# Retention products on the full 128x128 array, with one mask operation per head pair

## The chip, the cores and the metric

One core of a Trainium2 chip runs the whole program as one launch. The metric is device time in microseconds, the median of several runs. TensorE multiplies, VectorE (DVE), ScalarE (ACT) and GpSimd (POOL) do the elementwise work, and SyncE (SP) issues nearly all DMAs. TensorE's results land in PSUM, in banks of 512 fp32 columns.

## The reference, cut to what matters

A retention layer (a linear recurrence with one decay per head) feeds two FFNs in a row.

```python
batch, n_heads, seq, head_dim = (4, 8, 768, 64)
gamma = 1.0 - 2.0 ** (-5.0 - np.arange(H, dtype=np.float32))
for t in range(S):
    state = gamma[None, :, None, None] * state + np.einsum('bhd,bhe->bhde', k[:, :, t], v[:, :, t])
    y[:, :, t] = scale * np.einsum('bhd,bhde->bhe', q[:, :, t], state)
...
x = attn_out.transpose(0, 2, 1, 3).reshape(B * S, H * D)      # 3072 tokens of 512
h = x @ w_in;  g = where(h > 0, h, exp(min(h, 0)) - 1);  x = g @ w_out          # first FFN, 512 -> 2048 -> 512
h = x @ w_in2; g = P(h) / (Q(h) + 1e-6);                 out = g @ w_out2       # second FFN
```

The weights arrive as float64 words, which the kernel turns to fp32 itself.

## The kernel before, in words

**Retention in chunks.** Each sequence of 768 steps is cut into 6 chunks of C = 128, so there are 24 chunks. A chunk has 4 *items*, one for each pair of heads; item i is chunk i // 4, pair i % 4, 96 items in all. With two heads of 64 features, a pair fills the 128 partitions. For an item TensorE makes, all in fp32:

- the *kv sum* (L189): decayed keys times values of the pair, 128x128, of which the two diagonal 64x64 blocks are used; left out in the last chunk of a sequence;
- the *scores* (L196): for each head, keys times queries of its 64 partitions, so with half of the array's rows. The two heads write to two PSUM banks, `pa` and `pb`;
- the *state product* (L223): the state `St` of both heads (block diagonal) times the queries, into the output tile `so`; left out in the first chunk of a sequence;
- the *output products* (L225): for each head its values times its masked scores, into its 64 partitions of `so`, so with half of the array's columns.

Between scores and output VectorE masks the scores of each head (L209: times a decay per row, times the triangle). `at_state` updates `St` from the kv sum, and `at_x` splits `so` into a high and a low part, `xh` and `xl`, which are the FFN's input.

**Order.** It is written out by hand; each engine takes its instructions as they were emitted. First come 16 items alone (the *opening*, chunks 0 to 3), while the first weights are converted. Then the first FFN runs over NB = 6 token blocks j and KF = 16 slices f: twelve matmuls of 512 columns make `h` (`g1`), and twelve more accumulate into `acc` (`g2`, for the slice before). One item is woven into each of the first 80 of these steps: its state and output products stand behind `g1`, and the kv sum and scores of the next item behind `g2`. Block 0 converts the first FFN's weights on the way (L106 to L110 on VectorE, L120 on GpSimd); blocks 1 to 4 convert the second FFN's. Block 5 and the second FFN have no retention.

**Loads.** After the last item of a chunk has its scores, `load_k` issues keys, keys for the kv sum and values of the next chunk on SP (L152 to L154). From chunk 4 on, `kT` and `kn` have one buffer each and the values have two. GpSimd multiplies `kn` by its decay (`scale_k`, L163) before the next kv sum.

Of the kernel before, what the change touches and what calls it, by code (L numbers as in the profile page):

```python
# [17 lines left out]
H = 8  # L18
S = 768
D = 64  # L20
# [27 lines left out]
def retention_ffn_kernel(ctx: ExitStack, tc: tile.TileContext, qkT, kv, w1i, w1o, w2i, w2o, a_, b_, tab, out):  # L48
# [26 lines left out]

# [1 line left out]
    W = {}  # L77
# [36 lines left out]
    def split_w(ph, f, e):  # L114
        c = W.pop((ph, f, e, "c"))
        nm = "io"[e]
        hi = wp.tile([128, 512], F32R, tag=f"{nm}h{f}", name=f"{nm}h{f}")
        lo = wp.tile([128, 512], F32R, tag=f"{nm}l{f}", name=f"{nm}l{f}")
# [5 lines left out]
    tab_t = acon.tile([128, tab.shape[1]], F32, name="tab_t")  # L124
# [4 lines left out]
    tri_t = tab_t[:, 532:532 + C]  # L129
    St = acon.tile([128, NP, 128], F32, name="St")  # L130

    def chunk_bufs(alloc):
        kT, kn = alloc("kT"), alloc("kn")
        return kT.rearrange("p (a t) -> p a t", a=NP), kn.rearrange("p (h d) -> p h d", h=H)

    chk = {}

    def load_q(c):
        if c in (2, 3):
            qT, vn, kT, kn = (wp.tile([128, 512], F32, tag=next(late), name=nm) for nm in ("qT", "vn", "kT", "kn"))  # L140
            qT, kT = (t.rearrange("p (a t) -> p a t", a=NP) for t in (qT, kT))
            vn, kn = (t.rearrange("p (h d) -> p h d", h=H) for t in (vn, kn))
        else:
            qT = atw.tile([128, NP, C], F32, tag="qT", name="qT")
            vn = atw.tile([128, H, D], F32, tag="vn", name="vn")
            kT, kn = cb[1 if c == 1 else 0]
        nc.sync.dma_start(out=qT, in_=qkT[c, :, 0])
        chk[c] = (qT, vn, kT, kn)

    def load_k(c):  # L150
        qT, vn, kT, kn = chk[c]
        nc.sync.dma_start(out=kT, in_=qkT[c, :, 1])  # L152
        nc.sync.dma_start(out=kn, in_=kv[c, :, 0])
        nc.sync.dma_start(out=vn, in_=kv[c, :, 1])  # L154

    def scale_q(c, eng):
        qT, vn, kT, kn = chk[c]
        eng.tensor_tensor(out=qT, in0=qT, in1=gq_t, op=ALU.mult)

    def scale_k(c):  # L160
        qT, vn, kT, kn = chk[c]
        if c % CB != CB - 1:
# [12 lines left out]
    def at_in(i, early=False):  # L175
        c, p = divmod(i, NP)
        qT, vn, kT, kn = chk[c]
        if early:
            pa, pb = (psh.tile([128, 512], F32, tag="h", name="sc") if i % 3 == 2 else
                      psa.tile([128, 512], F32, tag=f"acc{2 * (i % 3) + e}", name="sc") for e in range(2))  # L180
        else:
            pa = pst.tile([128, 256], F32, tag="sc", name="sc")
            if p % 2 == 0:
                so_t[0] = pst.tile([128, 3, C], F32, tag="so", name="so")
            pb = so_t[0][:, 2, :]
        ps_t[i] = (pa, pb)
# [12 lines left out]

    def at_mask(i, early=False):  # L200
        p = i % NP
        if early and i % 2:
            A = wp.tile([128, 2, C], F32, tag="ih14", name="A1")
        else:
            A = atw.tile([128, 2, C], F32, tag="A", name="A", bufs=1)
        A_t[i] = A

        def part(e):
            nc.vector.scalar_tensor_tensor(out=A[:, e, :], in0=ps_t[i][e][:, 0:C], scalar=gi_t[:, 2 * p + e:2 * p + e + 1],  # L209
                                           in1=tri_t, op0=ALU.mult, op1=ALU.mult)  # L210

        return [lambda: part(0), lambda: part(1)]

    def at_out(i, early=False):
        c, p = divmod(i, NP)
        qT, vn, kT, kn = chk[c]
        A = A_t.pop(i)
        if early and p % 2 == 0:
            so_t[1] = (pst.tile([128, 3, C], F32, tag="so", name="so") if i % 4 else
                       pst.tile([128, 2, C], F32, tag="sc", name="so"))  # L220
        o = so_t[1 if early else 0]
        if c % CB:
            nc.tensor.matmul(out=o[:, p % 2, :], lhsT=St[:, p, :], rhs=qT[:, p, :], start=True, stop=False)  # L223
        for e in range(2):
            nc.tensor.matmul(out=o[64 * e:64 * e + 64, p % 2, :], lhsT=vn[:, 2 * p + e, :], rhs=A[:, e, :],  # L225
                             start=(c % CB == 0), stop=True)

    def at_state(i):
        c, p = divmod(i, NP)
        kv_ps = ps_t.pop(i)[0]  # L230

        def part(e):
            r = slice(64 * e, 64 * e + 64)
            src = kv_ps[r, C + 64 * e:C + 64 + 64 * e]
            dst = St[r, p, 64 * e:64 * e + 64]
# [9 lines left out]

    def at_x(i, early=False):
        c, p = divmod(i, NP)
        if p % 2:
            o = so_t[1 if early else 0]
            xh, xl = x_tile(c // 4)  # L250
# [35 lines left out]

# [1 line left out]
    def gemm3(ps, pairs, first, last):  # L288
# [66 lines left out]

# [1 line left out]
    ctx.enter_context(tc.manual_schedule())  # L357

    nc.scalar.preload_act_table_set("natural_log_exp_and_others")
    cb = [chunk_bufs(lambda nm: acon.tile([128, 512], F32, name=nm))]  # L360
    late = iter(("ih15", "il15", "ih13", "il13", "ih12", "il12", "ih11", "il11", "oh15", "ol15"))
    cb.append(chunk_bufs(lambda nm: wp.tile([128, 512], F32, tag=next(late), name=nm + "1")))
    nc.gpsimd.memset(St, 0.0)
# [17 lines left out]
    lnb = const.tile([128, 2], F32, name="lnb")  # L381
    warm = gp.tile([128, 512], F32R, tag="gl", name="warm")
    nc.vector.memset(warm.bitcast(F32), 0.0)
    wps = psa.tile([128, 512], F32, tag="acc0", name="wps")
    for _ in range(NW):
        nc.tensor.matmul(out=wps, lhsT=warm[:, 0:128], rhs=warm, start=True, stop=True)
    nc.vector.memset(lnb[:, 0:1], QC * TINY)
    nc.vector.memset(lnb[:, 1:2], -LN2_63)
    scale_q(0, nc.vector)
    scale_k(0)  # L390
    scale_q(1, nc.gpsimd)
    conv_ops = []
    for i in range(4 * NP):
        c, p = divmod(i, NP)
        at_in(i, True)
        a = at_mask(i, True)
        a[0]()
        if conv_ops:
            conv_ops.pop(0)()
        a[1]()  # L400
        if i:
            at_out(i - 1, True)
            run(at_state(i - 1))
            at_x(i - 1, True)
        if p == 0 and c:
# [14 lines left out]
    run(at_state(4 * NP - 1))  # L420
    at_x(4 * NP - 1, True)
    narrow_a(0, 1, 1)
# [18 lines left out]
    for j in range(NB):  # L441
        last = j == NB - 1
        for f in range(KF):
# [6 lines left out]
            x1 = narrow_b(0, f + 1, 1) if conv1 else [lambda: None] * 4  # L450
            a = at_mask(nx[0]) if not last else [lambda: None] * 2
            st = [lambda: None] * 2
# [6 lines left out]
            else:  # L459
                x2 = [lambda: None] * 4  # L460
            x1[0](), a[0](), x1[1](), a[1]()
            if not last:
# [47 lines left out]

# [1 line left out]
    at.close()  # L512
# [103 lines left out]
```

## Time and profile before

| | |
|---|---|
| median of 3 runs | 1241.63 us (1241.39 to 1242.66) |
| profiled execution: its span, first to last instruction | 1243.3 us |
| TensorE matmul busy | 1220.0 us, 98% of the span |
| VectorE busy | 800.3 us, 64% |
| ScalarE busy | 648.1 us, 52% |
| GpSimd busy | 420.0 us, 34% |
| mean granted TensorE clock | 0.991 |

Busy shares are means over stages with different limits. Matmul records overlap one another, so a full TensorE row says that it did not wait, not that the array streamed all the time. The profile gives no time outside the span for the profiled execution, which lies 1.7 us above the median of the runs.

### The profile page before, as it was taken

To read this page: it belongs to the slowest core of one execution; us is meant where nothing else is said; L and a number is where in the kernel's file an instruction comes from. 1 tells how busy PE (TensorE), PEld (TensorE's weight loads), DVE (VectorE), ACT (ScalarE), POOL (GpSimd) and SP (SyncE) were. 2 spreads that over 40 slices of the span, in tenths; PEclk is the share of its full clock that TensorE was granted. 3 is DMA by queue.
4 is the path that set the end of the run, shared out by engine and by line. 5 is a ranking of instruction groups with operands and counts; after the bars stand their busy time and mean duration, and the time that the engine had idled before them with its cause. 6 is when DMAs were issued, how large, how long until landed. Compare 5 with 4: busy or idle time off the path is not lost.

```text
span 1243.3 us, 15558 instructions
## 1 busy us (share of the span) xinstructions
PE 1220.0 (98%) x5708; PEld 969.9 (78%) x5708; DVE 800.3 (64%) x1348; ACT 648.1 (52%) x1098; POOL 420.0 (34%) x328
## 2 busy tenths in 40 slices
PE   9888899999999999999999999999999999999998
PEld 6666677777777777777788888888888888888887
DVE  6899964444444544445311188788888888888775
ACT  2444443333333333333345587776776776777665
POOL 3455542322222222232247743223233232233222
PEclk9899899999999999999999999999999999999999
DMA  6354422223332332322224320020020100100000
GB/s 238 120 170 153 153 98 99 85 89 125 110 110 86 126 103 85 119 85 85 102 94 119 106 73 1 1 69 1 1 69 1 54 15 1 60 9 1 34 1 35
DMA packets 41389, 95.73 MB, mean 77 GB/s; under 512 B 4704, under 2 KB 4832, under 8 KB 41312
## 3 DMA queue, kind: packets, MB, share of 16 engines
q1 hardware_dynamic: 41024, 94.39, 23.4%
q8 instruction: 45, 0.74, 0.2%
q10 hardware_dynamic: 288, 0.34, 0.1%
q14 instruction: 32, 0.26, 0.1%
HBM read 73.74 MB, written 20.97 MB: 76 GB/s over the span
## 4 chain that ended last, share of the span: by engine, by line
PE 91%; DVE 6%; issue 1%; DMA 0%; ACT 0%; SPq 0%
PE h L290 42%; PE acc L290 41%; PE sc L196 3%; PE so L225 3%; DVE wc L108 2%; PE sc L189 2%; DVE wc L110 1%; PE so L223 1%; DVE wc L106 1%; DVE wc L107 1%; DVE A L209 0%; DMA vn<-in_kv_dram 0%; DVE St L241 0%; DVE t L479 0%; PE so L196 0%
## 5 line engine op out<-in xcount | busy, mean ns | idle before, releaser
L290 PE MATMUL h<-xh,ih 128*128 128x512 f32 x768 | 310.8, 405 | 0.0
L290 PE MATMUL h<-xh,il 128*128 128x512 f32 x768 | 302.6, 394 | 0.0
L290 PE MATMUL h<-xl,ih 128*128 128x512 f32 x768 | 302.5, 394 | 0.0
L545 POOL TENSOR_TENSOR gl<-e,gh 128x512 fp32r<-128x512 f32 x96 | 124.9, 1301 | 350.0 <-ACT gh L544 212.0
L483 POOL TENSOR_TENSOR gl<-t,gh 128x512 fp32r<-128x512 f32 x96 | 123.5, 1286 | 348.7 <-ACT gh L482 295.8
L466 ACT ACTIVATE t<-h 128x512 f32<-128x512 f32 x96 | 57.4, 598 | 287.5 <-PE h L290 284.7
L290 PEld LDWEIGHTS h<-xh,ih 128*128 128x128 f32 x768 | 145.8, 190 | 38.1 <-ACT gh L482 0.2
L290 PEld LDWEIGHTS h<-xh,il 128*128 128x128 f32 x768 | 145.8, 190 | 31.2
L290 PEld LDWEIGHTS h<-xl,ih 128*128 128x128 f32 x768 | 146.1, 190 | 28.3
L290 PE MATMUL acc<-gh,oh 128*128 128x512 f32 x384 | 158.9, 414 | 0.0
L290 PE MATMUL acc<-gh,ol 128*128 128x512 f32 x384 | 150.5, 392 | 0.0
L290 PE MATMUL acc<-oh,gh 128*128 128x512 f32 x384 | 149.4, 389 | 0.0
L290 PE MATMUL acc<-ol,gh 128*128 128x512 f32 x384 | 149.4, 389 | 0.0
L519 ACT ACTIVATE s<-h 128x512 f32<-128x512 f32 x96 | 57.4, 598 | 136.9 <-PE h L290 136.9
L479 DVE SCALAR_TENSOR_TENSOR t<-t,h 128x512 f32<-128x512 f32 x96 | 65.5, 682 | 85.7 <-ACT t L467 84.9
L482 ACT CAST gh<-t 128x512 fp32r<-128x512 f32 x96 | 59.6, 621 | 103.9 <-DVE t L479 103.9
L209 DVE SCALAR_TENSOR_TENSOR A<-sc,tab_t 128x128 f32<-128x128 f32 x112 | 38.6, 348 | 111.2 <-PE so L196 106.6
L525 DVE SCALAR_TENSOR_TENSOR u<-s,b,u 128x512 f32<-128x512 f32 x96 | 72.0, 750 | 56.0 <-ACT u L520 55.4
L290 PE MATMUL acc<-gl,oh 128*128 128x512 f32 x384 | 103.4, 391 | 0.0
L290 PE MATMUL acc<-oh,gl 128*128 128x512 f32 x384 | 103.1, 389 | 0.0
L535 DVE SCALAR_TENSOR_TENSOR e<-e,ab,r 128x512 f32<-128x512 f32 x96 | 72.1, 751 | 32.0 <-ACT r L529 32.0
L290 PEld LDWEIGHTS acc<-gh,oh 128*128 128x128 f32 x384 | 72.0, 187 | 26.2 <-issue 13.5
(61 smaller groups left out, 2003.6 us busy)
## 6 DMA issues: line engine op xcount, KB each, us to landing
st<-in_w1i_dram SPq DMA_DIRECT2D x16, 512.0 KB, 3.5
st<-in_w1o_dram SPq DMA_DIRECT2D x16, 512.0 KB, 3.5
st<-in_w2i_dram SPq DMA_DIRECT2D x16, 512.0 KB, 5.4
w2s<-wc SPq DMA_DIRECT2D x32, 256.0 KB, 2.0
st<-in_w2o_dram SPq DMA_DIRECT2D x16, 512.0 KB, 3.6
wc<-w2s SPq DMA_DIRECT2D x32, 256.0 KB, 2.7
qT<-in_qkT_dram SPq DMA_DIRECT2D x24, 256.0 KB, 4.4
kT<-in_qkT_dram SPq DMA_DIRECT2D x24, 256.0 KB, 2.7
```

The costliest lines, as they stand in the source:

```text
L196: nc.tensor.matmul(out=ps[:, 0:C], lhsT=kT[r, p, :], rhs=qT[r, p, :], start=True, stop=True)
L209: nc.vector.scalar_tensor_tensor(out=A[:, e, :], in0=ps_t[i][e][:, 0:C], scalar=gi_t[:, 2 * p + e:2 * p + e + 1], in1=tri_t, op0=ALU.mult, ...
L225: nc.tensor.matmul(out=o[64 * e:64 * e + 64, p % 2, :], lhsT=vn[:, 2 * p + e, :], rhs=A[:, e, :], start=(c % CB == 0), stop=True)
L290: nc.tensor.matmul(out=ps, lhsT=lh, rhs=rh, start=first and idx == 0, stop=last and idx == len(pairs) - 1)
L466: nc.scalar.activation(out=t, in_=h, func=ACTF.Relu, scale=-1.0)
L479: nc.vector.scalar_tensor_tensor(out=t, in0=t, scalar=-1.0, in1=h, op0=ALU.add, op1=ALU.max)
L482: nc.scalar.copy(gh, t)
L483: nc.gpsimd.tensor_tensor(out=gl, in0=t, in1=gh.bitcast(F32), op=ALU.subtract)
L519: nc.scalar.activation(out=s, in_=ps, func=ACTF.Square)
L525: nc.vector.scalar_tensor_tensor(out=u, in0=s, scalar=b1, in1=u, op0=ALU.mult, op1=ALU.add)
L535: nc.vector.scalar_tensor_tensor(out=e, in0=e, scalar=ab[:, 0:1], in1=r, op0=ALU.add, op1=ALU.mult)
L545: nc.gpsimd.tensor_tensor(out=gl, in0=e, in1=gh.bitcast(F32), op=ALU.subtract)
```

## The change

Keys and values of a pair are kept in tiles twice as wide, in which each head has its own 128 columns (keys) or 128 rows' worth of columns (values), and the other head's half is zero. The zeros are written once, at the start (`wide_k` on GpSimd, `wide_v` on VectorE); the loads fill only the other parts, in two DMAs for the keys and two for the values, in place of one each. With them every product takes all 128 rows and columns: scores contract over 128 partitions, of which 64 are zero for the other head, and the two output products of a pair accumulate into the same 128 partitions. Both heads' scores stand side by side in one PSUM bank together with the kv sum, so that the mask of a pair is one operation of 128 x 256, by a table `mask` of 8 x 128 columns that is built once. The kv sum reads the values' two used parts out of the wide tile.

Also changed: the output tile is taken by `at_out` and not by `at_in`; the opening uses five PSUM banks for scores in turn, where it used three pairs; a weight's high and low part share one tile; ten more warm-up matmuls; a smaller scratch for dynamic DMA.

```diff
+    mask = acon.tile([128, H, C], F32, name="mask")
+
+    def wide_k(t):
+        t = t.rearrange("p (a e t) -> p a e t", a=NP, e=2)
+        for e in range(2):
+            r = slice(64 - 64 * e, 128 - 64 * e)
+            nc.gpsimd.memset(t[r, :, e, :], 0.0)
+        return t
+
+    def wide_v(t):
+        t = t.rearrange("p (a e d) -> p a e d", a=NP, e=2)
+        for e in range(2):
+            nc.vector.memset(t[:, :, e, 64 - 64 * e:128 - 64 * e], 0.0)
+        return t
...
     def load_k(c):
-        qT, vn, kT, kn = chk[c]
-        nc.sync.dma_start(out=kT, in_=qkT[c, :, 1])
+        qT, vw, kw, kn = chk[c]
+        for e in range(2):
+            r = slice(64 * e, 64 * e + 64)
+            nc.sync.dma_start(out=kw[r, :, e, :], in_=qkT[c, r, 1])
         nc.sync.dma_start(out=kn, in_=kv[c, :, 0])
-        nc.sync.dma_start(out=vn, in_=kv[c, :, 1])
+        for e in range(2):
+            nc.sync.dma_start(out=vw[:, :, e, 64 * e:64 * e + 64],
+                              in_=kv[c, :, 1].rearrange("p (a e) d -> p a e d", e=2)[:, :, e, :])
...
-                nc.tensor.matmul(out=pa[:, C:2 * C], lhsT=kn[:, 2 * p:2 * p + 2, :], rhs=vn[:, 2 * p:2 * p + 2, :],
+                v2 = vw[:, p].rearrange("p e d -> p (e d)").rearrange("p (f d) -> p f d", d=64)[:, 0:4:3, :]
+                nc.tensor.matmul(out=ps[:, 2 * C:3 * C], lhsT=kn[:, 2 * p:2 * p + 2, :], rhs=v2,
                                  start=True, stop=True)
...
-        for e, ps in enumerate((pa, pb)):
-            r = slice(64 * e, 64 * e + 64)
-            nc.tensor.matmul(out=ps[:, 0:C], lhsT=kT[r, p, :], rhs=qT[r, p, :], start=True, stop=True)
+        for e in range(2):
+            nc.tensor.matmul(out=ps[:, e * C:e * C + C], lhsT=kw[:, p, e, :], rhs=qT[:, p, :], start=True, stop=True)
...
-        def part(e):
-            nc.vector.scalar_tensor_tensor(out=A[:, e, :], in0=ps_t[i][e][:, 0:C], scalar=gi_t[:, 2 * p + e:2 * p + e + 1],
-                                           in1=tri_t, op0=ALU.mult, op1=ALU.mult)
-
-        return [lambda: part(0), lambda: part(1)]
+        nc.vector.tensor_tensor(out=A, in0=ps_t[i][:, 0:2 * C].rearrange("p (e t) -> p e t", e=2),
+                                in1=mask[:, 2 * p:2 * p + 2, :], op=ALU.mult)
...
         for e in range(2):
-            nc.tensor.matmul(out=o[64 * e:64 * e + 64, p % 2, :], lhsT=vn[:, 2 * p + e, :], rhs=A[:, e, :],
-                             start=(c % CB == 0), stop=True)
+            nc.tensor.matmul(out=o[:, p % 2, :], lhsT=vw[:, p, e, :], rhs=A[:, e, :],
+                             start=(c % CB == 0 and e == 0), stop=(e == 1))
...
+    for n in (256, 384):
+        for _ in range(5):
+            nc.tensor.matmul(out=wps[:, 0:n], lhsT=warm[:, 0:128], rhs=warm[:, 0:n], start=True, stop=True)
...
+    for h in range(H):
+        nc.vector.tensor_scalar_mul(mask[:, h, :], tri_t, gi_t[:, h:h + 1])
```

On TensorE, in one step of block 0 (each step of blocks 1 to 4 reads alike), an item stands so before; one row of the two FFN products is shown at each border.

```order
L290 MATMUL acc_606<-gl,oh_387 128x512
L189 MATMUL sc<-vn,kn 128x128
L196 MATMUL sc<-qT,kT 128x128
L196 MATMUL so<-qT,kT 128x128
L290 MATMUL h<-xh,ih_538 128x512
...
L223 MATMUL so<-qT,St 128x128
L225 MATMUL so<-A,vn 64x128 x2
L290 MATMUL acc_603<-gh,oh_521 128x512
```

And so after the change, where k_136, v_137 and n_139 are the wide keys, the wide values and the keys of the kv sum:

```order
L298 MATMUL acc_598<-gl,wo_397 128x512
L201 MATMUL sc<-v_137,n_139 128x128
L207 MATMUL sc<-qT,k_136 128x128 x2
L298 MATMUL h<-xh,wi_534 128x512
...
L231 MATMUL so<-qT,St 128x128
L233 MATMUL so<-A,v_137 128x128 x2
L298 MATMUL acc_595<-gh,wo_518 128x512 x2
```

The number of calls and their places are the same; the output products have 128 rows where they had 64, and both scores go to `sc`.

On SP, the first chunk's loads and the start of the next chunk's before:

```order
L147 DMA qT<-in_qkT_dram 128x512
L152 DMA kT<-in_qkT_dram 128x512
L153 DMA kn<-in_kv_dram 128x512
L154 DMA vn<-in_kv_dram 128x512
L147 DMA qT<-in_qkT_dram 128x512
```

And after; x2 is two DMAs:

```order
L156 DMA qT<-in_qkT_dram 128x512
L162 DMA k_136<-in_qkT_dram 64x4x128 x2
L163 DMA n_139<-in_kv_dram 128x512
L165 DMA v_137<-in_kv_dram 128x4x64 x2
L156 DMA qT<-in_qkT_dram 128x512
```

The keys of the kv sum stand one DMA later, and the second half of the values two DMAs later.

## Rows read from the trace of the kernel before

**Rows 1.** Page: the chain that ended last, shares by engine.

```profile
PE 91%; DVE 6%; issue 1%; DMA 0%; ACT 0%; SPq 0%
```

**Rows 2.** Busy time by stretch: opening, block 0, blocks 1 to 4.

```profile
core 0: us, PE busy (x) PEld busy (x) DVE busy (x) ACT busy (x) POOL busy (x), PEclk, DMA share, GB/s
8.00:36.00 28.00, 26.28 (x178) 17.06 (x178) 25.27 (x71) 7.12 (x21) 12.26 (x10) 1.00 0.61 220
...
46.00:160.00 114.00, 99.62 (x452) 73.49 (x450) 110.23 (x167) 55.37 (x99) 63.66 (x45) 0.94 0.46 143
165.00:625.00 460.00, 460.00 (x2302) 356.42 (x2301) 211.12 (x472) 153.34 (x269) 118.82 (x95) 1.00 0.31 102
```

**Rows 3.** Chain in order of time (start us, us), one item, block 1.

```profile
171.74 2.96 PE acc L290 x12
174.71 0.22 PE sc L189 x2
174.93 0.30 PE sc L196
...
175.24 0.11 PE sc L196
175.35 2.95 PE h L290 x12
178.30 0.22 PE so L223 x2
178.52 0.37 PE so L225 x4
```

**Rows 4.** The same chain where retention has ended.

```profile
624.58 2.96 PE acc L290 x12
627.54 2.72 PE h L290 x12
630.26 2.72 PE acc L290 x12
```

**Rows 5.** Timeline at a chunk's border (start us, us, engine, line), block 1.

```profile
365.70 0.38 PE L189 MATMUL sc<-vn,kn 128*128 128x128 f32 x2
...
366.02 0.37 PE L196 MATMUL sc<-qT,kT 64*128 64x128 f32 x1
...
366.02 0.37 PE L196 MATMUL so<-qT,kT 64*128 64x128 f32 x1
...
366.54 0.35 DVE L209 SCALAR_TENSOR_TENSOR A<-sc,tab_t 128x128 f32<-128x128 f32 x1 [2.06 <-PE so L196]
...
366.81 0.34 DVE L209 SCALAR_TENSOR_TENSOR A<-so,tab_t 128x128 f32<-128x128 f32 x1
...
367.43 0.42 SPq L154 DMA_DIRECT2D vn<-in_kv_dram  x1
...
370.65 1.05 POOL L163 TENSOR_TENSOR kn<-kn,tab_t 128x512 f32<-128x512 f32 x1 [4.16 <-DMA kn<-in_kv_dram]
...
372.85 0.38 PE L189 MATMUL sc<-vn,kn 128*128 128x128 f32 x2
```

**Rows 6.** DMA issues from 170 to 620 us: count, KB, us to landing.

```profile
vn<-in_kv_dram SPq DMA_DIRECT2D x15, 256.0 KB, 4.6
```

**Rows 7.** DMA queues from 1 to 6 us: packets, MB, share of 16 engines.

```profile
q1 hardware_dynamic: 547, 1.01, 64.0%
...
q10 hardware_dynamic: 288, 0.34, 23.2%
```

**Rows 8.** Group by line and shape: busy us, mean ns, idle before.

```profile
L253 DVE TENSOR_TENSOR xl<-so,xh 128x256 fp32r<-128x256 f32 x48 | 20.3, 423 | 57.7 <-ACT xh L252 57.4
```

**Rows 9.** Timeline of the first 9 us.

```profile
1.45 5.46 PE L386 MATMUL wps<-warm 128*128 128x512 f32 x12 [1.45 <-DVE lnb L388]
...
6.26 1.04 POOL L163 TENSOR_TENSOR kn<-kn,tab_t 128x512 f32<-128x512 f32 x1 [5.00 <-DMA kn<-in_kv_dram]
...
8.39 0.61 DVE L209 SCALAR_TENSOR_TENSOR A<-sc,tab_t 128x128 f32<-128x128 f32 x2 [3.05 <-PE sc L189]
```

More of the change, by code (lines that the diff above doesn't have):

```diff
@@ L116, in split_w @@
         nm = "io"[e]
-        hi = wp.tile([128, 512], F32R, tag=f"{nm}h{f}", name=f"{nm}h{f}")
-        lo = wp.tile([128, 512], F32R, tag=f"{nm}l{f}", name=f"{nm}l{f}")
+        w = wp.tile([128, 2, 512], F32R, tag=f"{nm}{f}", name=f"w{nm}{f}")
+        hi, lo = w[:, 0, :], w[:, 1, :]
         nc.scalar.copy(hi, c)
@@ L139, in load_q @@
         if c in (2, 3):
-            qT, vn, kT, kn = (wp.tile([128, 512], F32, tag=next(late), name=nm) for nm in ("qT", "vn", "kT", "kn"))
-            qT, kT = (t.rearrange("p (a t) -> p a t", a=NP) for t in (qT, kT))
-            vn, kn = (t.rearrange("p (h d) -> p h d", h=H) for t in (vn, kn))
-        else:
[L144 to L148, printed above, removed]
+            qT = half[c][:, 512:1024]
+        else:
+            qT = atw.tile([128, 512], F32, tag="qT", name="qT")
+        chk[c] = (qT.rearrange("p (a t) -> p a t", a=NP),) + kvb[c if c < 4 else ("even", "odd")[c % 2]]
+        nc.sync.dma_start(out=chk[c][0], in_=qkT[c, :, 0])
     def load_k(c):
-        qT, vn, kT, kn = chk[c]
-        nc.sync.dma_start(out=kT, in_=qkT[c, :, 1])
+        qT, vw, kw, kn = chk[c]
+        for e in range(2):
+            r = slice(64 * e, 64 * e + 64)
+            nc.sync.dma_start(out=kw[r, :, e, :], in_=qkT[c, r, 1])
         nc.sync.dma_start(out=kn, in_=kv[c, :, 0])
-        nc.sync.dma_start(out=vn, in_=kv[c, :, 1])
+        for e in range(2):
+            nc.sync.dma_start(out=vw[:, :, e, 64 * e:64 * e + 64],
+                              in_=kv[c, :, 1].rearrange("p (a e) d -> p a e d", e=2)[:, :, e, :])
     def scale_q(c, eng):
-        qT, vn, kT, kn = chk[c]
+        qT = chk[c][0]
         eng.tensor_tensor(out=qT, in0=qT, in1=gq_t, op=ALU.mult)
     def scale_k(c):
-        qT, vn, kT, kn = chk[c]
+        kn = chk[c][3]
         if c % CB != CB - 1:
@@ L176, in at_in @@
         c, p = divmod(i, NP)
[L177 to L180, printed above, removed]
-        else:
[L182 to L186, printed above, removed]
+        qT, vw, kw, kn = chk[c]
+        if not early or i % 5 == 4:
+            ps = pst.tile([128, 512], F32, tag="sc", name="sc")
+        elif i % 5 < 3:
+            ps = psa.tile([128, 512], F32, tag=f"acc{i % 5}", name="sc")
+        else:
+            ps = psh.tile([128, 512], F32, tag="h", name="sc")
+        ps_t[i] = ps
         def kv_sum():
             if c % CB != CB - 1:
-                nc.tensor.matmul(out=pa[:, C:2 * C], lhsT=kn[:, 2 * p:2 * p + 2, :], rhs=vn[:, 2 * p:2 * p + 2, :],
+                v2 = vw[:, p].rearrange("p e d -> p (e d)").rearrange("p (f d) -> p f d", d=64)[:, 0:4:3, :]
+                nc.tensor.matmul(out=ps[:, 2 * C:3 * C], lhsT=kn[:, 2 * p:2 * p + 2, :], rhs=v2,
                                  start=True, stop=True)
@@ L359, in retention_ffn_kernel, with late, heads @@
     nc.scalar.preload_act_table_set("natural_log_exp_and_others")
-    cb = [chunk_bufs(lambda nm: acon.tile([128, 512], F32, name=nm))]
-    late = iter(("ih15", "il15", "ih13", "il13", "ih12", "il12", "ih11", "il11", "oh15", "ol15"))
-    cb.append(chunk_bufs(lambda nm: wp.tile([128, 512], F32, tag=next(late), name=nm + "1")))
+    warm = gp.tile([128, 512], F32R, tag="gl", name="warm")
+    nc.vector.memset(warm.bitcast(F32), 0.0)
+    def late(tag):
+        return wp.tile([128, 1024], F32, tag=tag, name="l" + tag)
+    def heads(t):
+        return t.rearrange("p (h d) -> p h d", h=H)
+    k0, v0, v1 = (acon.tile([128, 1024], F32, name=nm) for nm in ("k0", "v0", "v1"))
+    n0 = acon.tile([128, 512], F32, name="n0")
+    half = {c: late(tag) for c, tag in ((1, "o15"), (2, "i13"), (3, "o12"))}
+    kvb = {0: (wide_v(v0), wide_k(k0), heads(n0))}
+    kvb[1] = (wide_v(v1), wide_k(late("i15")), heads(half[1][:, 0:512]))
+    kvb[2] = (wide_v(late("o14")), wide_k(late("i14")), heads(half[2][:, 0:512]))
+    kvb[3] = (wide_v(late("i12")), wide_k(late("o13")), heads(half[3][:, 0:512]))
+    kvb["even"] = kvb[0]
+    kvb["odd"] = (kvb[1][0],) + kvb[0][1:]
     nc.gpsimd.memset(St, 0.0)
@@ L420, in retention_ffn_kernel @@
     run(at_state(4 * NP - 1))
-    at_x(4 * NP - 1, True)
+    at_x(4 * NP - 1)
     narrow_a(0, 1, 1)
@@ L450, in retention_ffn_kernel @@
             x1 = narrow_b(0, f + 1, 1) if conv1 else [lambda: None] * 4
-            a = at_mask(nx[0]) if not last else [lambda: None] * 2
             st = [lambda: None] * 2
@@ L460, in retention_ffn_kernel @@
                 x2 = [lambda: None] * 4
-            x1[0](), a[0](), x1[1](), a[1]()
+            x1[0]()
+            if not last:
+                at_mask(nx[0])
+            x1[1]()
             if not last:
```

36 lines of the change are left out of this document (15 added, 21 removed).

## The prediction

> **What bounds the kernel now.** I read the chain of waits first. Matmuls hold 91% of it and VectorE 6% [rows 1], so the question is where each of the two ends last. The table by stretches answers it. From 165 to 625 us (token blocks j = 1 to 4, where 64 retention items run between the products) TensorE is busy for 460.00 of 460 us and VectorE for less than half. From 46 to 160 us (block 0, where weights are converted) VectorE is busy for 110.23 of 114 us and TensorE has gaps; in the first 36 us (16 retention items alone) VectorE is also nearly full [rows 2]. After 625 us nothing of the change is left. So three stages want three sums: TensorE time in blocks 1 to 4, VectorE time in block 0 and in the opening.
>
> What retention costs TensorE in blocks 1 to 4 can be read off the chain piece by piece: two records of the kv sum take 0.22 us, the scores 0.30 + 0.11, the state product 0.22, the two output products 0.37; and the twelve matmuls of each FFN product take 2.96 and 2.95 us [rows 3]. As soon as retention has ended, the same twelve take 2.72 us [rows 4]. So a FFN product that follows a retention product starts with some 0.23 us in which nothing is streamed, and that is as much as a whole state product. The reader should see that the two long pieces hide the largest part of the overhead.
>
> **TensorE in blocks 1 to 4.** The state product and the kv sum use the whole array already, and their two records take 0.22 us, 0.11 each [rows 3]. After the change all of retention has that form: per item 2 records for the kv sum, 4 for the scores, 2 for the state product, 4 for the output, since one call is two records. If no product has to wait at a border between forms, an item costs 12 x 0.11 = 1.32 us beside 2 x 2.72 = 5.44 us, against 7.13 now (the sum of [rows 3]). The first score pair shows what is given up: both heads start together, at 366.02 [rows 5], which full-array products can't do. Yet the scores take 0.41 us with that overlap and 4 x 0.11 = 0.44 without it; the output 0.37 and 0.44. The overlap is worth 0.10 us per item; the two slow starts of the FFN products are worth 0.47.
> For the stage: 64 items lie between the acc piece at 171.74 and that at 624.58 [rows 3, 4], 452.84 us. Three chunks of four items have no kv sum (the last of a sequence) and three no state product (the first), so the records are 40 x 12 + 24 x 10 = 720. After: 64 x 5.44 + 720 x 0.11 = 427.4 us. **Term 1: -25.4 us.** Bounds: 0.107 per record would give -27.6; that the slow start stays is a rival below.
> Of the slow start the row shows only that it is there between half-array fp32 products and full-array FFN products. The Trainium skill (TensorEngine Tiling (Array Packing), Key Properties) says that a change of the tiling mode drains TensorE; this trace agrees as far as it goes, and by that rule all of the 0.47 us goes. What the page says against the change stands at rival 4.
>
> **Loads of a chunk.** This is what the change adds. Keys come as two DMAs and values as two, so a chunk is six instead of four, and the runs get shorter: 512 bytes for the keys, 256 for the values. They are issued on SP behind the last scores of the chunk before. Now: the last item of a chunk starts at 365.70, the values are issued at 367.43, and they land 4.6 us after issue (median [rows 6]), at 372.0, for a kv sum that starts at 372.85 [rows 5]: 0.8 us to spare. The decayed keys are ready at 370.65 + 1.05 = 371.7, 1.1 us to spare. After: two more issues of 0.43 us stand ahead of the second half of the values (+0.86), the item is 0.4 us shorter, the scores end 0.05 us sooner. The spare time of the values is 0.8 - 0.86 - 0.4 + 0.05 = -0.4 us before shorter runs cost anything; that of the keys, +0.3.
> What the runs cost is not in the trace, so I bound it. In 5 us of the opening, a packet of q1 (1.01 MB / 547 = 1.85 KB) took 0.64 x 16 x 5 / 547 = 0.094 us, one of q10 (1.18 KB in the mean) 0.232 x 16 x 5 / 288 = 0.064 [rows 7]. Below: bytes alone, no cost. Above: every short packet costs 0.064; the 1,024 of the values then take 1,024 x 0.064 / 16 = 4.1 us instead of 128 x 0.094 / 16 = 0.75, 3.3 us later. A straight line through the two rows puts a packet of 256 bytes near 0.022: 1.4 us for the values, 0.65 more than now. Each half is on its way while the next is issued, so I count the second half of that, 0.2 to 0.3. TensorE meets the values first in the new item (the kv sum leads), with scores, FFN product and everything behind them in order, so the wait is on the path. It falls on the chunks whose kv sum exists and whose spare time is the short one of blocks 1 to 4: 16 less 3, 13 chunks. **Term 2: 13 x 0.6 = +8 us** (0 to 13 x 3.7 = 48).
>
> **VectorE in block 0 and in the opening.** The two mask operations of an item take 0.35 us each, but the second starts 0.27 after the first [rows 5], so 0.53 together. One operation of 128 x 256 with an input from PSUM and one from SBUF is what writes xl: 0.42 us [rows 8], 0.34 if the next may start as much earlier. Saved: 0.19 us per item, bounds 0.11 and 0.28. Block 0: 16 x 0.19 = 3.0; from it I take 1 us, since SP sits behind weight loads there and three chunks arrive later still. **Term 3: -2 us.** Opening: items 4 to 15 are paced by VectorE, 12 x 0.19 = -2.3. Against it stands the longer warm-up: 3,200 more columns beside 12 x 512 = 6,144 that took 5.46 us [rows 9], so 2.8 us at that rate and 1.4 at twice the clock; the first four items are paced by TensorE and get 1 us shorter. **Term 4: -1 us** (-3 to +2). Hidden there: eight mask products and eight clears of the value tiles on VectorE, which has little to do before its first mask at 8.39 [rows 9]; eight clears of key tiles on GpSimd, for which the first kn at 6.26 us leaves room [rows 9] (without that cover each would cost about as much as the 0.42 us of xl). Weight tiles joined in one, other PSUM banks for scores, and the output tile taken later cost nothing: TensorE never waits for them in blocks 1 to 4, where its row shows no idle time.
>
> **Sum.** -25.4 + 8 - 2 - 1 = -20 us. The profiled execution has a span of 1243.3 us and lies 1.7 us above the median of the runs, 1241.6; I take the same difference off the median: 1221 us.
>
> **Rivals.**
> 1. *The values come too late* (the other side). Place: the kv sum that opens each of 13 chunks. For it: the spare time is used up by issue alone. Against it: DMA engines are idle for two thirds of the stage (share 0.31 [rows 2]), so only latency counts. At the upper bound 48 us replace 8: 1261 us. It decides from about 28.4 / 13 = 2.2 us of wait per chunk.
> 2. *The slow start belongs to the change from fp32 to the FFN's type*, not to the half array. No row has a full-array fp32 product followed by an FFN product, so this is open; against it, the other direction (h to the state product, acc to the kv sum) shows no gap: 2 records in 0.22 us [rows 3]. Then 64 x 0.47 = 30 us stay: 1251 us. It ends slower than now from 20 / 128 = 0.16 us a start.
> 3. *Every fp32 call starts slowly*, half array or not. The first score pair takes 0.30 us where the second takes 0.11 [rows 3]; if that 0.19 belongs to any call behind an fp32 call, the 360 calls of the stage need 427.4 + 360 x 0.19 = 495.8 us, 43 more than now: 1241.6 + 43 + 8 - 3 = 1290 us. No row has two full-array calls one behind the other; against it stands the kv sum, which opens without loss behind a FFN product.
> 4. *Scores and outputs double*, as the pair that ran together now runs one after the other: 0.41 + 0.37 more per item [rows 3], 64 x 0.78 = 50 us, of which the starts give back 30: 1241.6 + 20 + 8 - 3 = 1267 us. Against it, the state product has twice the array's rows of a score and takes 0.22, not 0.41 [rows 3]. The Trainium skill (TensorEngine Tiling (Array Packing), Theoretical Speedup) has such a rule: at 64 rows or less tiling gives up to twice the speed. The trace agrees that pairs overlap [rows 5], not that they are that fast.
> 5. *The clock falls in the opening.* TensorE gets 1.32 us of work for an item that VectorE paces at some 1.9, so its gaps grow; the granted clock was 0.94 in block 0, where TensorE has gaps, and 1.00 in the stages where it has few or none [rows 2]: part of block 0 ran at 1.2 instead of 2.4 GHz. At 1.2 GHz an item takes 2.64 us of TensorE: 12 x 0.75 = 9 us: 1230.
> 6. *The edit does not do what it says*: the diff's order of instructions shows the full-array products and one mask per pair, so I give it nothing.
>
> **Chances.** Forecast with waits up to 1.4 us per chunk, 1209 to 1232: 0.70. Clock: 0.08. Values late enough to spoil it: 0.10, of which 0.04 ends within 0.2%. Slow start stays: 0.07. Every call slow: 0.03. Doubled: 0.02. A difference of 0.2% (2.5 us) is about what a measurement of this kernel can tell. Faster: 0.70 + 0.08 = 0.78; same 0.04; slower 0.18. The low end is no wait at all and 4 us more from the other stages: 1209. The high end leaves out rivals 2 to 4 and most of 1: 1244.
>
> **What would show it.** Right: an item of 6.7 to 6.8 us in blocks 1 to 4, both twelves near 2.72 us, L207 and L233 at 0.44. A wait of L201 for the values, four items apart, is term 2; if it is absent, the gain is 25 us or more. Twelves still at 2.95 would be rival 2, a score pair above 0.6 us rival 3 or 4, a clock under 1 before 36 us rival 4. VectorE's mask should be one operation of 0.34 to 0.45 us. I would be wrong if items shorten and the total does not.

## The result, and the profile after

The median is 1228.28 us in four runs (1226.19 to 1232.88), against 1242.14 for the kernel before, measured beside it (1241.39 to 1243.80): a ratio of 0.989, 95% interval 0.987 to 0.991. The forecast was 1221, its range 1209 to 1244. The execution profiled is the fastest of the four, 1226.19 us with a span of 1224.4, so the two profiles differ by 18.9 us where the medians differ by 13.9.

The stages can be cut at the moment when ScalarE first touches h of a block (start us, us, engine, line, operation). Before, for blocks 0, 1 and 5:

```profile
43.91 0.60 ACT L466 ACTIVATE t<-h 128x512 f32<-128x512 f32 x1 [5.70 <-PE h L290]
...
178.40 0.60 ACT L466 ACTIVATE t<-h 128x512 f32<-128x512 f32 x1 [3.17 <-PE h L290]
...
630.36 0.60 ACT L466 ACTIVATE t<-h 128x512 f32<-128x512 f32 x1 [3.04 <-PE h L290]
```

And after:

```profile
42.03 0.60 ACT L492 ACTIVATE t<-h 128x512 f32<-128x512 f32 x1 [2.54 <-PE h L298]
...
175.87 0.60 ACT L492 ACTIVATE t<-h 128x512 f32<-128x512 f32 x1 [1.52 <-PE h L298]
...
611.46 0.60 ACT L492 ACTIVATE t<-h 128x512 f32<-128x512 f32 x1 [2.91 <-PE h L298]
```

| stage | before | after | change | predicted |
|---|---|---|---|---|
| opening, to the first h | 43.91 | 42.03 | -1.9 | -1 |
| block 0 | 134.49 | 133.84 | -0.65 | -2 |
| blocks 1 to 4 | 451.96 | 435.59 | -16.4 | -25.4 + 8 = -17.4 |
| the rest | 612.94 | 612.94 | 0 | 0 |

So the gain is where the prediction put it, in blocks 1 to 4. There the chain, which answers to [rows 3, 4], reads so for an item and, at its end, where retention is over (the row at 605.90 follows the last output products):

```profile
176.44 2.75 PE acc L298 x12
179.20 0.22 PE sc L201 x2
179.42 0.45 PE sc L207 x4
179.86 2.75 PE h L298 x12
182.62 0.22 PE so L231 x2
182.84 0.45 PE so L233 x4
...
605.90 2.75 PE acc L298 x12
608.65 2.72 PE h L298 x12
```

The gap at the scores has gone, both twelves (the twelve matmuls of an FFN product) are 0.20 us shorter, and an item takes 6.84 us from one h to the next instead of 7.14 (medians of blocks 1 to 4). The busy time by stretch, beside [rows 2]:

```profile
core 0: us, PE busy (x) PEld busy (x) DVE busy (x) ACT busy (x) POOL busy (x), PEclk, DMA share, GB/s
8.00:36.00 28.00, 23.23 (x182) 21.02 (x181) 20.72 (x53) 6.99 (x20) 11.79 (x10) 1.00 0.87 231
...
46.00:160.00 114.00, 95.33 (x456) 77.58 (x456) 111.92 (x157) 55.33 (x99) 66.79 (x45) 0.96 0.45 142
165.00:625.00 460.00, 458.61 (x2372) 388.25 (x2372) 202.91 (x410) 160.99 (x283) 126.45 (x100) 1.00 0.33 106
```

TensorE is no longer full from 165 to 625 us: 1.4 us of gaps stand out there. VectorE has room in the opening now (20.72 of 28 us) but none in block 0, although its mask work there fell. What TensorE waits for in the new gaps, from 170 to 620 us (engine, line, waited for: us in all, times, longest):

```profile
PEld sc L201 <- POOL n L175: 3.3, 7, 0.9
PE sc L201 <- DMA v<-in_kv_dram: 1.4, 3, 0.5
```

Their sum is more than TensorE's gap, since the row of the weight loads (PEld) waits while the last matmuls still run. These are the kv sums that open a chunk, as predicted, but they wait more often for the keys that GpSimd decays (n) than for the values (v).

### The profile page after: what moved, and what is told of

Same layout as the page of the kernel before. It is cut to its first block, busy times and chain, and to the rows that moved or that the text cites. A ratio compares the mean times of both kernels' runs of the same rounds, so it can differ in the third digit from the quotient of the medians.

```text
span 1224.4 us, 15508 instructions
## 1 busy us (share of the span) xinstructions
PE 1191.1 (97%) x5718; PEld 995.2 (81%) x5718; DVE 790.2 (65%) x1268; ACT 647.6 (53%) x1098; POOL 431.4 (35%) x336
## 4 chain that ended last, share of the span: by engine, by line
PE 86%; DVE 9%; DMA 2%; issue 1%; SPq 1%; ACT 0%; POOL 0%; POOLq 0%
PE acc L298 39%; PE h L298 39%; DVE wc L108 3%; PE sc L207 3%; PE so L233 2%; DVE wc L110 2%; DVE wc L106 2%; PE sc L201 1%; DVE wc L107 1%; DMA v<-in_kv_dram 1%; PE so L231 1%; DMA st<-in_w1o_dram 1%; DVE St L249 1%; DVE t L505 1%; DMA k<-in_qkT_dram 0%
## 5 line engine op out<-in xcount | busy, mean ns | idle before, releaser
L298 PE MATMUL h<-xh,wi 128*128 128x512 f32 x1536 | 514.7, 396 | 0.0
L298 PEld LDWEIGHTS h<-xh,wi 128*128 128x128 f32 x1536 | 290.3, 189 | 58.9
L298 PE MATMUL h<-xl,wi 128*128 128x512 f32 x768 | 300.7, 392 | 0.0
L298 PE MATMUL acc<-gh,wo 128*128 128x512 f32 x768 | 199.8, 402 | 0.0
L298 PE MATMUL acc<-wo,gh 128*128 128x512 f32 x768 | 190.2, 389 | 0.0
L298 PEld LDWEIGHTS acc<-wo,gh 128*128 128x128 f32 x768 | 144.2, 188 | 29.9
L298 PEld LDWEIGHTS h<-xl,wi 128*128 128x128 f32 x768 | 145.4, 189 | 28.1
L298 PEld LDWEIGHTS acc<-gh,wo 128*128 128x128 f32 x768 | 139.4, 190 | 26.3
L298 PE MATMUL acc<-wo,gl 128*128 128x512 f32 x384 | 103.1, 389 | 0.0
L298 PE MATMUL acc<-gl,wo 128*128 128x512 f32 x384 | 102.9, 390 | 0.0
```

The source lines that it names most:

```text
L298: nc.tensor.matmul(out=ps, lhsT=lh, rhs=rh, start=first and idx == 0, stop=last and idx == len(pairs) - 1)
```

## The experiments

All are edits of the changed kernel (after the change), and ratios are against the kernel before.

### The two borders, one at a time

Half-array scores again from the first FFN on, and in another run half-array outputs again:

```diff
             # half_scores: second score into so_t[0][:, 2, :], two masks
-    lhsT=kw[:, p, e, :], rhs=qT[:, p, :]
+    lhsT=kw[r, p, e, :], rhs=qT[r, p, :]                      # r = the head's 64 partitions
             # half_out
-    out=o[:, p % 2, :], lhsT=vw[:, p, e, :], start=(c % CB == 0 and e == 0), stop=(e == 1)
+    out=o[r, p % 2, :], lhsT=vw[:, p, e, r], start=(c % CB == 0), stop=True
```

> The changed kernel, but from the first FFN on (blocks 0 to 4) the two scores of an item are again two half-array products into two banks, with a mask operation each; outputs stay on the full array. Theory (the slow start of a FFN product belongs to the border from half-array products): the twelve behind the scores goes from 2.75 back to 2.95 us, the one behind the outputs stays at 2.75; the scores go from 0.45 to 0.41; 0.16 us more per item, some 10 us in blocks 1 to 4, and 2 to 3 us in block 0 for the second mask operation: 1239 to 1242 us. Rival (the gain came from what else the edit moved: banks, the output tile, joined weight tiles): both twelves as they are or both back at 2.95; at 2.75 the time stays near 1230.

> The changed kernel, but from the first FFN on the two output products of an item are again half-array products, into the upper and the lower half of the output's partitions; scores stay on the full array with one mask. Theory (border between forms): the twelve behind the outputs goes from 2.75 to 2.96, the one behind the scores stays at 2.75; the outputs go from 0.45 to 0.37; 0.13 us more per item, 8 us in blocks 1 to 4, nothing in block 0, which VectorE sets: 1235 to 1238 us. Rival (the start belongs to fp32 products or to the banks): the acc twelve stays at 2.75, and the time falls by 64 x 0.08 = 5 us to 1223.

Measured: 1240.37 us, ratio 0.998 (0.997 to 0.999), with half-array scores; 1234.45 us, 0.993 (0.991 to 0.995), with half-array outputs. The chain of the first and then of the second:

```profile
178.31 0.45 PE so L244 x4
178.76 2.75 PE acc L309 x12
...
181.73 0.30 PE sc L213
...
182.15 2.95 PE h L309 x12
```

```profile
181.04 0.37 PE so L238 x4
181.41 2.96 PE acc L303 x12
...
184.59 0.45 PE sc L207 x4
185.04 2.75 PE h L303 x12
```

Each twelve goes back to 2.95 or 2.96 exactly when the products ahead of it are half-array ones, and the other stays at 2.75. So the slow start belongs to that border. In the second run nothing but the form of the outputs changed, so banks, output tile and joined weight tiles have no part in it there; the first run also puts the second score into another bank again, so for the scores the bank is not separated from the form. Items take 7.01 and 6.97 us, against 6.84, and blocks 1 to 4 are 12.6 and 6.8 us longer, where I expected some 10 and 8; the second total lies just below its range. The extra 2 to 3 us that I expected of a second mask in block 0 did not show: block 0 took 134.05 us.

### What is left of the slow start

```diff
+        if i > 32:                      # no kv sum, no scores from here on
+            ps_t[i] = ps_t["kept"]
+            return
```

> The changed kernel, but from the second item of block 1 on the kv sum and the two scores are left out (the mask reads old scores), so that the products of the first FFN follow the acc twelve directly. Theory (the 0.03 us that a twelve takes in excess of the 2.72 it takes with no retention is what a border from fp32 products to the FFN's type costs on any array form): the h twelve, now behind a FFN product, takes 2.72 us, the acc twelve, behind the outputs, stays at 2.75; an item 6.84 - 0.67 - 0.03 = 6.14. Rival (the 0.03 belongs to something else in these blocks, such as the loads of weights or the second FFN's conversions beside it): both stay at 2.75, an item 6.17.

Measured: an item of 6.14 us (1182.28 us in all), with this chain:

```profile
200.35 0.45 PE so L238 x4
200.80 2.75 PE acc L303 x12
203.55 2.72 PE h L303 x12
```

A FFN product behind a FFN product takes 2.72 us, one behind full-array fp32 products 2.75, one behind half-array ones 2.95. The step from full-array fp32 products to the FFN's type costs 0.03 us, in the other direction nothing that these rows show.

### What is late at a chunk's border

The keys of the kv sum as they are loaded, before GpSimd decays them, are called natural keys here. They are issued first:

```diff
+        nc.sync.dma_start(out=kn, in_=kv[c, :, 0])
         for e in range(2):
             ...
             nc.sync.dma_start(out=kw[r, :, e, :], in_=qkT[c, r, 1])
-        nc.sync.dma_start(out=kn, in_=kv[c, :, 0])
```

> The changed kernel with one change of order: of a chunk's loads the natural keys (which GpSimd still has to decay) are issued before the two key pieces, so 1.2 us sooner; the values stay where they are, last. Theory (what is late at a chunk's border is the decayed keys, not the values): the waits of the kv sum for GpSimd's decayed keys, 3.3 us in blocks 1 to 4, go, those for values stay at 1 to 2 us, and blocks 1 to 4 get 2 us shorter, to 433.5; total 1226. Rival (the values are as late as the keys, and the last of the two only took the name): the waits move to the values, and blocks 1 to 4 stay at 435 to 436.

Measured: 1224.31 us (1223.29 to 1224.57), ratio 0.985 (0.984 to 0.987). From 165 to 600 us TensorE is busy for 435.00 of 435 us, and blocks 1 to 4 take 433.3 us. At one border the loads stand so, in the changed kernel and then with the natural keys first (start us, us, SP's issues; the kv sum last):

```profile
274.77 1.29 SPq L162 DMA_DIRECT2D k<-in_qkT_dram  x2
...
276.12 0.59 SPq L163 DMA_DIRECT2D n<-in_kv_dram  x1
...
276.76 0.97 SPq L165 DMA_DIRECT2D v<-in_kv_dram  x2
...
281.59 0.46 PE L201 MATMUL sc<-v,n 128*128 128x128 f32 x2 [0.43 <-DMA v<-in_kv_dram]
```

```profile
272.98 0.42 SPq L160 DMA_DIRECT2D n<-in_kv_dram  x1
...
275.03 1.30 SPq L163 DMA_DIRECT2D k<-in_qkT_dram  x2
...
276.39 1.15 SPq L165 DMA_DIRECT2D v<-in_kv_dram  x2
...
281.26 0.38 PE L201 MATMUL sc<-v,n 128*128 128x128 f32 x2
```

The natural keys go out 3.1 us sooner, not 1.2: their buffer is free as soon as the last kv sum has read it, and they had been standing in SP's queue behind the key pieces, which wait for the scores. What SP waits for from 165 to 600 us, in the changed kernel and then here (us in all, times, longest):

```profile
SPq L162 <- PE sc L207: 53.2, 16, 16.4
```

```profile
SPq L160 <- PE sc L201: 43.6, 14, 16.0
```

The values gained 0.4 us too, and that was enough for them, so the run doesn't separate keys and values as sharply as I meant it to: the waits for the decayed keys were the more frequent ones, and both vanish.

### Issues or short runs

The value tile as value, zeros, value, zeros, so that one DMA fills it; in a second kernel together with the keys first:

```diff
-        for e in range(2):
-            nc.sync.dma_start(out=vw[:, :, e, 64 * e:64 * e + 64], in_=...[:, :, e, :])
+        nc.sync.dma_start(out=vw.rearrange("p (h d) -> p h d", h=H)[:, :, 0:D], in_=kv[c, :, 1])
```

> The changed kernel with the zeros shared between neighbours: value, zeros, value, zeros along the row, so that a chunk's values are one DMA (64 of every 128 elements) in place of two; the number and size of short runs is the same. Theory (in the opening the first weights are late because SP issues one DMA after the other, at 0.4 to 0.6 us each; the runs cost little): SP reaches the first weights 0.9 us and the fourth load 2 us sooner, the first FFN activation moves from 42.0 to 40 to 41.5 us, blocks 1 to 4 stay at 435 to 436: 1226 to 1227. Rival (the runs cost, the issues do not): nothing changes, or the single DMA lands later than the halves (3.3 us), near 4.6, and the kv sum waits some 1 us more for values at 13 borders, 1240.

> Both edits of the loads together on the changed kernel: the natural keys first, and the values as one DMA. Theory: the waits at the chunk borders are gone (as with the keys first alone, 433.3 us in blocks 1 to 4) and the opening is shorter by up to 1.5 us: 1222 to 1224. Rival (the two save the same time): 1224 to 1225, no faster than with the keys first alone.

Measured: 1226.38 us, 0.985 (0.980 to 0.989), alone; 1224.51 us, 0.983 (0.979 to 0.986), with the keys first, no faster than the keys first alone in another comparison (1224.31). (The kernel before spread from 1240.67 to 1255.95 us in this comparison, which widens the intervals.) Alone, the first h comes at 41.20 instead of 42.03 us, as the theory had it but within the 40.8 to 44.1 of kernels with one and the same opening, and blocks 1 to 4 take 435.0. The values in one DMA land 3.8 us after issue, in the same 256-byte runs; in whole rows they took 4.6 [rows 6]. The key pieces, half the bytes each, land after 2.8 us (medians from 170 to 620 us), where whole keys took 2.7; the queries, which follow in the same queue with their rows unchanged, after 5.4 instead of 4.4. So the short runs do not make the values visibly later; what they cost the keys, and whether they hold up the queries behind them, was not tested. What they cost the queue, the page shows of before and of after, with the same bytes (packets, MB, share of 16 engines over the span):

```profile
q1 hardware_dynamic: 41024, 94.39, 23.4%
```

```profile
q1 hardware_dynamic: 72512, 94.40, 24.8%
```

That is 16 x (0.248 x 1224.4 - 0.234 x 1243.3) = 204 us more of engine time for 31,488 more packets, 0.0065 us for each that was added, and in blocks 1 to 4 the share is 0.33 in the mean and below 0.6 in each of 40 slices.

### The longer warm-up

```diff
-    for n in (256, 384):
-        for _ in range(5):
-            nc.tensor.matmul(out=wps[:, 0:n], lhsT=warm[:, 0:128], rhs=warm[:, 0:n], ...)
```

> The changed kernel without the ten matmuls that the edit added to the warm-up. Theory: they only fill the time until the first keys have landed, so the first scores start no sooner than now (8.45 us, at the earliest 0.5 us before), the granted clock of the opening stays 1.00 from 8 to 36 us, and the time stays within 2 us of the changed kernel's. Rival (they keep the clock up): with a gap before the first scores the granted clock falls to half in the opening, the first items take up to twice as long, and the opening gets 2 us or more longer; or (they are in the way) the opening gets 1 us shorter, as the prediction charged them.

Measured: 1227.75 us, 0.987 (0.981 to 0.993), the same as with it.

```profile
6.63 1.03 PE L207 MATMUL sc<-qT,k 128*128 128x128 f32 x4
9.16 0.64 PE L201 MATMUL sc<-v,n 128*128 128x128 f32 x2 [1.50 <-DMA v<-in_kv_dram]
```

Both theories missed a part. The first scores do start sooner, at 6.63 instead of 8.45 us, but then TensorE waits 1.5 us for the first values. Behind that gap the granted clock falls to 1.2 GHz for a while (0.50 from 10 to 12 us; 0.94 in the mean from 8 to 36 us, against 1.00). The first h still comes at 41.69 us instead of 42.03, so the loss does not reach it.

### Block 0: two masks, the mask twice

```diff
             # two_masks, everywhere: the old form on the new tile, for e in range(2)
+    nc.vector.scalar_tensor_tensor(out=A[:, e, :], in0=ps_t[i][:, e * C:e * C + C], scalar=gi_t[...], in1=tri_t, ...)
             # mask_twice, in block 0
+    for _ in range(2):
         nc.vector.tensor_tensor(out=A, in0=ps_t[i][:, 0:2 * C]..., in1=mask[:, 2 * p:2 * p + 2, :], op=ALU.mult)
```

> The changed kernel with full-array products everywhere, but each pair is masked by two operations of the old form (128x128, a scalar per row times the triangle) in place of one multiplication by the mask table. The prediction's theory: VectorE is nearly full in the opening and in block 0 and is paid 0.19 us per item, so the opening is longer by 2 us and block 0 by 2 to 3 us, blocks 1 to 4 stay at 435.6: 1232 us. Rival (the opening and block 0 wait for loads and for SP's issues, so VectorE's saving is swallowed there): opening and block 0 change by less than 0.7 us each, time 1228.

> The changed kernel, but in block 0 each item's mask multiplication is issued twice in a row (the second writes the same values again). Theory A (block 0 lasts as long as VectorE's operations added up, as the prediction had it): 16 more operations that start 0.34 us apart make block 0 longer by 5.4 us, 133.8 to 139.2. Theory B (what fills VectorE in block 0 is its own work plus the time in which GpSimd's operations hold up conversions between SBUF tiles; the mask reads PSUM, and GpSimd runs beside it, so a longer mask takes waiting time away from the conversions): the conversions get shorter by most of what the masks add, and block 0 grows by 1 to 2.5 us.

Measured: 1231.37 us, 0.991 (0.989 to 0.992), with two masks; 1229.19 us, 0.990 (0.988 to 0.991), with the mask twice. Block 0 takes 134.82 and 137.76 us, against 133.84: 1.0 us for two masks, where the prediction's 0.19 per item would make 3.0, and no more than kernels with one mask differ by (133.7 to 135.1); 3.9 us for the mask twice, between the two theories (5.4, and 1 to 2.5). With two masks the first h comes at 46.10 us, but there the granted clock was 0.66 from 36 to 46 us and 1.00 in the changed kernel's profile, so how much of the 4.1 us is the mask's stays open.

VectorE's groups in block 0 say more. Masks plus the four conversion operations (L106 to L110) are busy for 10.9 + 101.9 = 112.8 us before, 6.7 + 106.3 = 113.0 after, 9.7 + 101.6 = 111.3 with two masks and 13.1 + 101.3 = 114.4 with the mask twice. These stretches hold 112, 115, 112 and 115 conversions, so one takes 0.910, 0.924, 0.907 and 0.881 us. The mask twice adds 6.4 us of masks, and the same 115 conversions give up 5.0. From before to after the masks give up 4.2 us; 1.6 of it goes into longer conversions, the rest into three more of them. Kernels with the same masks range from 0.886 to 0.940, so before and after alone would not show this. In the changed kernel's timeline one sees how:

```profile
88.97 0.41 DVE L106 TENSOR_SCALAR wc<-wc 128x512 f32<-128x512 f32 x1
89.31 0.41 DVE L219 TENSOR_TENSOR A<-sc,mask 128x256 f32<-128x256 f32 x1
89.64 0.41 DVE L107 TENSOR_SCALAR wc<-wc 128x512 int32<-128x512 int32 x1
90.08 1.67 DVE L108 SCALAR_TENSOR_TENSOR wc<-st,wc 128x512 int32<-128x512 int32 x1
91.68 1.51 DVE L106 TENSOR_SCALAR wc<-wc 128x512 f32<-128x512 f32 x1
```

with GpSimd beside it:

```profile
89.83 1.37 POOL L509 TENSOR_TENSOR gl<-t,gh 128x512 fp32r<-128x512 f32 x1 [2.26 <-issue]
91.17 1.74 POOL L120 TENSOR_TENSOR wi<-wc,wi 128x512 fp32r<-128x512 f32 x1
```

L106 takes 0.41 us alone and 1.51 when it starts while a GpSimd operation runs; L108 takes 0.69 and 1.67. Each ends 0.3 to 0.6 us after that GpSimd operation does. Of the 115 conversions of the block, 43 take 1.2 us or more and the others 0.70 or less. The mask, which reads PSUM, and the operation on t, which reads h there, keep their times wherever they stand (0.41 to 0.42 and 0.67 to 0.69). The Trainium skill (SBUF — State Buffer, SBUF: two separate sides) says that VectorE and GpSimd share one pair of SBUF ports under an exclusive lock, taken by VectorE's operations in a two-port mode, or with two SBUF inputs if GpSimd's operation reads SBUF (these do), and that the loser waits for the whole instruction. This trace agrees: about 1.0 us per meeting.

### Taking GpSimd out of block 0

If GpSimd's operations hold up the conversions in this way, then moving GpSimd's subtractions to the engine that is full must make block 0 shorter. Low parts of the weights first, then the low part of the activations as well; both kernels also issue the natural keys first:

```diff
     def split_w(ph, f, e, late_lo=False):
-        nc.gpsimd.tensor_tensor(out=lo, in0=c, in1=hi.bitcast(F32), op=ALU.subtract)
+        def sub_lo(eng):
+            eng.tensor_tensor(out=lo, in0=c, in1=hi.bitcast(F32), op=ALU.subtract)
+        if late_lo:                     # block 0
+            return lambda: sub_lo(nc.vector)
+        sub_lo(nc.gpsimd)
             # emitted behind the operation on t (out weights), and behind the next item's mask (in weights)
             # gl_vector: gl in block 0 by nc.vector too, behind the next item's mask
```

> The natural keys first, and in block 0 the low part of each split weight tile (29 subtractions of 128x512 that GpSimd does in 1.5 to 1.74 us) is computed by VectorE, placed where its inputs are ready. Theory A (VectorE is the bound of block 0 by its own work): 29 operations of 0.6 to 0.7 us more, block 0 gets 17 to 20 us longer, 1242. Theory B (each GpSimd operation holds up one conversion by some 1.0 us, 0.69 to 1.67): 29 such delays go and 29 operations of 0.69 come, block 0 gets 5 to 10 us shorter, 124 to 129, and the time falls to 1215 to 1220.

> As the kernel with the low parts of the weights on VectorE in block 0, and there the low part of the activations (gl, 15 subtractions of 128x512, which GpSimd does in 1.35 us while one subtraction of VectorE is held up from 0.68 to 1.32) is VectorE's as well, one item later. Theory B (a GpSimd operation costs VectorE 0.7 to 1.0 us, its own operation 0.6): block 0 gets 1 to 6 us shorter than the 121.7 us there, and the operations of VectorE on weights all take 0.7 us or less but for those beside q's scaling and the keys' decay. Theory A (VectorE pays its own work alone): 15 x 0.6 = 9 us longer.

Measured: 1211.91 us, 0.976 (0.974 to 0.977); with gl as well 1210.61 us, 0.975 (0.973 to 0.976). Block 0 takes 121.7 and 120.0 us. VectorE's groups there, in the changed kernel and then with the weights' low parts on VectorE (busy us, mean ns):

```profile
L108 DVE SCALAR_TENSOR_TENSOR wc<-st,wc 128x512 int32<-128x512 int32 x29 | 33.7, 1161 | 1.0
L110 DVE SCALAR_TENSOR_TENSOR wc<-st,wc 128x512 int32<-128x512 int32 x29 | 32.9, 1134 | 0.2
```

```profile
L110 DVE SCALAR_TENSOR_TENSOR wc<-st,wc 128x512 int32<-128x512 int32 x29 | 20.6, 711 | 0.2
L108 DVE SCALAR_TENSOR_TENSOR wc<-st,wc 128x512 int32<-128x512 int32 x29 | 20.1, 693 | 1.0
L123 DVE TENSOR_TENSOR wi<-wc,wi 128x512 fp32r<-128x512 f32 x14 | 18.5, 1323 | 0.0
...
L123 DVE TENSOR_TENSOR wo<-wc,wo 128x512 fp32r<-128x512 f32 x15 | 10.3, 684 | 0.0
```

VectorE does 29 more operations and is done 12 us sooner: the 115 conversions take 69.0 us instead of 106.3, and the operations that it takes on 28.8. Low parts that came late can hardly be the reason: in the changed kernel's block 0 the chain is made of VectorE's conversions for 63%, and no line of GpSimd has more than 1.8% of it. The subtraction for wo takes 0.68 us; the one for wi meets gl on GpSimd and takes 1.32. With gl moved both take 0.684. Block 0 is 1.7 us shorter then, about as much as kernels with the same block 0 differ by, and the two intervals overlap, so the gain of that second step is not shown.

## Why the prediction was right, and where it was off

The direction and the stage were right, but two errors of 6 us hid one another.

- **Term 1 (-25.4 us): right in mechanism, too large.** Without waits at the borders (the natural keys first) blocks 1 to 4 take 433.3 us, 18.7 less than 451.96. The step that was mis-sized is "2 x 2.72 = 5.44 us": behind full-array fp32 products a twelve is 2.75, which is 0.06 per item or 3.8 us, and scores and outputs take 0.45 and not 0.44, 1.3 us more. That makes 432.5 us in place of 427.4; the last 0.8 us are open, and 0.9 comes from the start of the sum, 452.84 where the stage table has 451.96. I took the value without retention for the one behind full-array retention; no row of before had that border.
- **Term 2 (+8 us): right place, too large.** The waits cost 435.6 - 433.3 = 2.3 us. The spare times were the wrong way round in part: I gave the decayed keys +0.3 us and the values -0.4, yet the kernel waits 7 times for the keys and 3 times for the values. For the values I kept the 4.6 us from issue to landing [rows 6] and added 0.2 to 0.3 for the short runs; in fact 128 KB halves land 3.3 us after issue. Against that, an issue took 0.49 to 0.65 us in the lines above, where I took 0.43. An added short packet costs 0.0065 us; my line through [rows 7] gave 0.65 x 16 / (1,024 - 128) = 0.012. What I did not read is that in SP's queue the natural keys stand behind pieces that wait for the scores.
- **Term 3 (-2 us): the step failed.** Block 0 got 0.65 us shorter, and kernels with the same block 0 took 133.7 to 135.1, so no gain is shown there. The step that failed is "16 x 0.19 = 3.0": a saving on VectorE is not passed on whole, since the conversions, held up by GpSimd, give way to longer masks and fill the place of shorter ones (5.0 of 6.4 us with the mask twice). How the missing 2 us of this change divide is open, as kernels with the same masks differ by as much. The steps "0.19 us per item" and "VectorE is busy for 110.23 of 114 us" were both right; the time of a conversion was not a constant. That GpSimd's operations hold up the conversions is shown by moving the subtractions; that it is a lock for the whole instruction no run shows by itself, but the ends of the long operations fit it. Of the 3.9 us that the mask twice cost, 2.1 are VectorE's busy time (125.93 us against 123.86) and the rest its idle time, which is not explained.
- **Term 4 (-1 us): in the range.** -1.9 us in the profiled execution, with a granted clock of 1.00 from 36 to 46 us where the kernel before had 0.66. Between kernels with the same opening the first h came at 40.8 to 44.1, so I can't split this into mask and clock. The parts that I named (-2.3, -1, and 1.4 or 2.8 for the warm-up) add up to -1.9 or -0.5, so -1 was a guess between them. The longer warm-up costs nothing that can be measured: the time is spent waiting for values otherwise.
- **Rivals.** Values far too late (1) and every call slow (3) or doubled (4) are refuted by the chain above. Rival 2 is refuted in its size: the type's part is 0.03 of 0.23 us. Scores and outputs lose 0.04 + 0.08 us per item by giving up the overlap. The Trainium skill's rule (TensorEngine Tiling (Array Packing), Theoretical Speedup: up to twice at 64 rows), taken at its full factor, would have made them lose 0.41 and 0.37, an estimate; in this trace tiling gained a pair 10 to 20% and cost the next product 0.20 us. Rival 5 came out the other way: the clock of the opening was not lower. (Its sign, a clock under 1 before 36 us, stands under rival 4's name in "What would show it".)
- **The sum** of -20 was made for one profiled execution and came out at -18.9 between the two profiles. The medians differ by 5 us less, and that comes from which executions were profiled. In all runs on record the time is 1.7 to 1.9 us above the span of the same execution, so the span of 1243.3 us stands for about 1245.1 us: 3 us above the median of its kernel (3.5 above the 1241.63 of the three runs, and not 1.7, which set a span against a time). The changed kernel's profiled execution is 2.1 us below its median. The changed kernel's runs spread over 6.7 us, with the natural keys first over 1.3 us; that fits waits that differ from run to run, but I did not test it.

## What to carry to other kernels

Count what a change of array form costs the next product, not only what it gives its own: here a pair gained 0.04 to 0.08 us by sharing the array and the long product behind it lost 0.20. A busy engine's row is not a sum of fixed durations: look for one operation with two durations, and at who runs beside the long one, before pricing a saving there. A DMA that waits for its buffer holds back all that stands behind it in its queue, so issue first what is free first.

## What was unexpected

The subtractions moved from GpSimd, which was busy for 77 of block 0's 134 us, to VectorE, which was full, made the block 12 us shorter (121.7; the keys' order, which that kernel has too, leaves it at 134.1 alone). The lowest median of this study is that kernel's with gl moved too: 1210.61 us, 32 us below the kernel before. And the values, loaded in shorter runs, landed sooner after their issue (3.3 and 3.8 us against 4.6), not later.
